# Layer 1 of a four-layer transformer stack: keys' feature map in one VectorE operation, and tiles 8 to 15 turned by crossbar DMAs

## The chip, the core and the metric

The kernel runs on one core of a Trainium2 chip. A core has TensorE (PE, the matrix unit), VectorE (DVE), ScalarE (ACT), GpSimd (POOL), SyncE (SP, which here issues every DMA) and 16 DMA engines. The metric is the time of one execution on the device in microseconds (us), as the median of a few runs.

## The reference

Four layers follow each other: A, B, A, B, with the same weights for both A layers and for both B layers. S = 2048 tokens, D = 576, H = 32 heads of 18, F = 4608, bf16 inputs.

```python
def _A_ref(x, wqkv, wo):                       # linear attention
    q, k, v = split_heads(x @ wqkv)
    phi = lambda t: jnp.where(t > 0, t + 1, jnp.exp(t)) + 1e-6
    pq, pk = phi(q), phi(k)
    kv = jnp.einsum("bhsd,bhse->bhde", pk, v)
    z = jnp.einsum("bhsd->bhd", pk)
    num = jnp.einsum("bhqd,bhde->bhqe", pq, kv)
    den = jnp.einsum("bhqd,bhd->bhq", pq, z)[..., None] + 1e-6
    return merge_heads(num / den) @ wo

def _B_ref(x, w1, b1, w2, b2):                 # MLP with its own layernorm
    h = _gelu(jnp.einsum("bsd,df->bsf", _layernorm(x), w1) + b1)
    return jnp.einsum("bsf,fd->bsd", h, w2) + b2

x = x + _A_ref(_layernorm(x), A_wqkv, A_wo)
x = x + _B_ref(_layernorm(x), B_w1, B_b1, B_w2, B_b2)
x = x + _A_ref(_layernorm(x), A_wqkv, A_wo)
x = x + _B_ref(_layernorm(x), B_w1, B_b1, B_w2, B_b2)
```

## The kernel before

The tokens are cut into 16 tiles of 128 (NT = 16). A tile of normalized rows is needed twice in an A layer. Turned (features on the partitions), it lies in `yT`, 5 chunks of 128 features by 2048 tokens, and feeds the projections to queries and keys. Unturned it is the stationary operand of the sums over tokens: instead of forming the values, the kernel sums rows times keys (`k2`, and a row of ones gives z) and multiplies by the value weights afterwards.

Layer 1 (li = 0) goes over the tiles in a loop written out by hand. `keys(t)` is two `k_half` calls, each 5 matmuls of 288 columns into PSUM. `pre_a1(t)` feeds a later tile to the layernorm pipe and ticks it. Then come one `q_proj` (5 matmuls of 512 columns) and `rows_by_keys(t, 0)` (5 matmuls: 4 chunks of rows into the accumulators accA and accB, and the tail of 64 features with the ones). TensorE's order is the order of the program, fixed by a chain of dependencies (`pe`). The order on DVE and ACT for the first tiles is written out (`in_order`, with names such as n0, ma00, e00, ca0).

The layernorm pipe (`LNPipe.tick`) takes each fed tile one stage further per tick: statistics (L397, L398 and L404 on DVE), variance plus epsilon (L415), the reciprocal root by a power on POOL (L433), minus mean times that (L436), the normalization (L444 on POOL from tile 4 on, L449 on DVE before), and stage 4, the turning. In layer 1 stage 4 is 5 TensorE transposes into PSUM (L500) and a copy to `yT` by ACT (L505). The last 64 features of a normalized tile are written to a ring of their own, `v_ring`, that has the ones beside them (`first_tail`), so a tile takes two normalizing operations. Tile t is fed in iteration t - 3 and turned in iteration t - 1.

The keys' feature map exists in two forms. `phi_from_psum` has two ACT passes (Exp at L554, Identity with a bias of 1 + 1e-6 at L555) and two DVE operations (L560, L562). `phi_by_dve` has one ACT pass (L537) and two DVE operations (L539, L541). The first half of the keys takes the first form, the second half the other.

All DMAs are issued by SP. In the beginning `chained` fixes their order: rows of x, the weights of layer 1, then `late_pieces` (w1 in 9 pieces with two tails each, wo, w2 in 6 pieces, b1), one piece per iteration in program order. A DMA waits on SP until the DMA eight before it has landed, and for the producer of its data.

In layers 2 and 4 (class `LayerB`) and in layer 3 nothing of this loop is used: rows are turned there by DVE in blocks of 32 and by DMAs through DRAM (`turn_rows`, `land`, L310, L325), and the unturned rows of layer 3 are loaded from DRAM (`load_row`, with the tails apart at L333). The loop of layer 3 has the same matmuls per tile (two `k_half`, one `q_proj`, one `rows_by_keys`) and no transposes.

Of the kernel before, what the change touches and what calls it, by code (L numbers as in the profile page):

```python
# [8 lines left out]
ALU = mybir.AluOpType  # L9
# [11 lines left out]
G = 5  # L21
# [9 lines left out]
HALF = D // 2  # L31
LAST_PARTS = (slice(0, 3 * P), slice(3 * P, D))
# [3 lines left out]
def build(tc, A_x, A_wqkv, A_wo, B_w1, B_b1, B_w2, B_b2, out, dbg=None, n_layers=4):  # L36
    nc = tc.nc
    dbg = dbg or {}
    with ExitStack() as ctx:
# [95 lines left out]
        NV = 2  # L135
        v_ring = [const.tile([P, G, P], BF16, name=f"v_ring{i}") for i in range(NV)]
        AHEAD = 4
        turned = const.tile([P, D // 32, TPC, 32], BF16, name="turned")
# [8 lines left out]
        def row_tile(name):  # L147
            return rows.tile([P, D], F32, name=name, tag="row")

        x0_tiles = {}  # L150

# [32 lines left out]
        def load_x0(t):  # L184
            if t % 2 == 0:
                x0_tiles["pair"] = rows.tile([P, 2, D], BF16, name="x0", tag="row")
            x0 = x0_tiles["pair"][:, t % 2, :]
            chained(nc.sync.dma_start(out=x0, in_=x_in[t * P:(t + 1) * P, :]))
            x0_tiles[t] = x0
# [31 lines left out]
        for vr in v_ring:  # L221
            nc.gpsimd.memset(vr[:], 0.0)
            nc.gpsimd.memset(vr[:].rearrange("p g c -> p (g c)")[:, 0:520].rearrange("p (t e) -> p t e", e=65)[:, :, 64:65], 1.0)
# [5 lines left out]
        def piece_w1(i):  # L229
            cs = slice(i * 512, (i + 1) * 512)  # L230
            chained(nc.sync.dma_start(out=w1_sb[:, 0:4, cs], in_=B_w1[0:4 * P, cs].rearrange("(k p) n -> p k n", p=P)))
            ts = slice(i * 256, (i + 1) * 256)
            for par in range(2):
                chained(nc.sync.dma_start(
                    out=w1_tail[64 * par:64 * (par + 1), ts].rearrange("k (f p) -> k f p", p=P),
                    in_=B_w1[4 * P:D, cs].rearrange("k (f two p) -> k f two p", two=2, p=P)[:, :, par, :]))
# [16 lines left out]
        def bias_casts():  # L253
# [4 lines left out]
                      [(lambda i=i: piece_w1(i)) for i in range(4, 9)] + [(lambda i=i: piece_w2(i)) for i in range(6)] + [piece_b1_dma]  # L258
# [6 lines left out]

        def tail_of(t):

            flat = v_ring[t // 8][:].rearrange("p g c -> p (g c)")
            return flat[:, (t % 8) * 65:(t % 8 + 1) * 65]

        def tails(c):
            flat = v_ring[c // 2][:].rearrange("p g c -> p (g c)")
            return flat[:, (c % 2) * 260:(c % 2 + 1) * 260].rearrange("p (t e) -> p t e", e=65)

        def first_tail(t, width=65):

            slot = 2 * (t % 8) + t // 8
            flat = v_ring[slot // 8][:].rearrange("p g c -> p (g c)")
            return flat[:, (slot % 8) * 65:(slot % 8) * 65 + width]
# [9 lines left out]
        def load_row(t):  # L289
            if t % 2 == 0:  # L290
                pair = rows.tile([P, 2, D], BF16, name="yrow_pair", tag="row")
                row_of[t], row_of[t + 1] = pair[:, 0, :], pair[:, 1, :]
            load = nc.sync.dma_start(out=row_of[t][:, 0:4 * P], in_=yrow_d[t // TPC, t % TPC].rearrange("j r d -> (j r) d")[:, 0:4 * P])
            if t >= 6:
                behind(load, "landed")
# [20 lines left out]
        def land(now=False):  # L316

            for it in list(landing):
# [11 lines left out]
                if kind == "A":  # L330
                    if c == NCB - 1:
                        sp_last["landed"] = landed.ins.name
                    tail = nc.sync.dma_start(out=tails(c)[:, :, 0:64],  # L333
                                             in_=yrow_d[c].rearrange("i j r d -> (j r) i d")[:, :, 4 * P:D])
                    behind(tail, "landed")
# [11 lines left out]
        class LNPipe:  # L347
# [11 lines left out]
            def tick(self, transposes=1):  # L359
                land()  # L360
                for it in list(self.items):
                    st = it["stage"]
                    if st == 4 and it["evac"] != "dma":
# [12 lines left out]
                    elif st == 0 and it["stats"] == "act":  # L376
# [7 lines left out]
                        continue  # L384
                    elif st == 0.5:
# [4 lines left out]
                        nc.gpsimd.tensor_scalar(out=u[:], in0=mv[:, 1:2], scalar1=(1.0 + EPS) / D, scalar2=EPS * EPS,  # L390
# [48 lines left out]
                    elif st in (2, 3) and it["kind"] == "A" and it["evac"] == "act":  # L439
                        xt, t = it["xt"], it["t"]  # L440
                        tail = first_tail(t)[:, 0:64]
                        if it["norm"] == "pool":
                            for out, cols in ((xt[:, 0:4 * P], slice(0, 4 * P)), (tail, slice(4 * P, D))):
                                norm = nc.gpsimd.tensor_scalar(out=out, in0=xt[:, cols], scalar1=it["rstd"][:, 0:1],  # L444
                                                               scalar2=it["nmr"][:, 0:1], op0=ALU.mult, op1=ALU.add)
                            pool_last["norm"] = norm.ins.name
                        else:
                            for name, out, cols in ((f"n{t}", xt[:, 0:4 * P], slice(0, 4 * P)), (f"nt{t}", tail, slice(4 * P, D))):
                                norm = named(name, nc.vector.tensor_scalar(  # L449
                                    out=out, in0=xt[:, cols], scalar1=it["mv"][:, 0:1], scalar2=it["rstd"][:, 0:1],  # L450
                                    op0=ALU.subtract, op1=ALU.mult))
# [31 lines left out]
                    elif st == 4:  # L483
                        t = it["t"]
                        first_layer = it["kind"] == "A" and it["evac"] == "act"
                        y = it["xt"] if first_layer else it["y"]
                        if it["evac"] == "dma":
                            turn_rows(y, t, it["kind"])
                            self.items.remove(it)
# [8 lines left out]
                        for k in range(KD):  # L498
                            block = first_tail(t, P) if first_layer and k == 4 else y[:, k * P:(k + 1) * P]
                            pe(nc.tensor.transpose(out=(tp if k < 3 else tp2)[:, k, :], in_=block, identity=ident[:]))  # L500
# [34 lines left out]
        def phi_by_dve(ps_ap, out_ap, rows, n, tag=None):  # L535
# [8 lines left out]
            if tag is not None:  # L544
                named("e" + tag, exp), named("mi" + tag, low), named("ma" + tag, top)

# [68 lines left out]
        def layer_A(li, next_kind, pre_a1=None):  # L615
# [34 lines left out]
            def k_half(t, half, defer=False):  # L650
# [5 lines left out]
                by_dve = half or li == 0 and t == 2  # L656

                def phi():
                    if (half, t // 2) not in self_k["pk"]:
                        self_k["pk"][(half, t // 2)] = blk.tile([P, D], BF16, name="pk", tag="blk")  # L660
                    pk = self_k["pk"][(half, t // 2)][:, (t % 2) * HALF:(t % 2 + 1) * HALF]
                    (phi_by_dve if by_dve else phi_from_psum)(kp[:, 0:HALF], pk, P, HALF,
                                                              tag=f"{t}{half}" if li == 0 and t < 4 else None)
                if defer:
                    return phi
                phi()

            def rows_by_keys(t, half, chunks=(4, 0, 1, 2, 3), done=True):
# [5 lines left out]
                pk = self_k["pk"][(half, t // 2)][:, (t % 2) * HALF:(t % 2 + 1) * HALF]  # L674
                for k in chunks:
                    dst = self_k["tail"][0:65, 0:HALF] if k == 4 else self_k["acc"][k // 2][:, k % 2, 0:HALF]
                    lhsT = (tail_of(t) if li > 0 else first_tail(t)) if k == 4 else row_of[t][:, k * P:(k + 1) * P]
                    pe(nc.tensor.matmul(dst, lhsT=lhsT, rhs=pk, start=(t == 0), stop=(t == NT - 1)))  # L678
                cols = slice(half * HALF, (half + 1) * HALF)
                if 4 in chunks and t == NT - 1:  # L680
                    nc.gpsimd.memset(zk[:, cols], 0.0)
                    nc.scalar.copy(out=k2[4][0:64, cols], in_=self_k["tail"][0:64, 0:HALF])
                    nc.scalar.copy(out=zk[64:65, cols], in_=self_k["tail"][64:65, 0:HALF])
                if not done:
                    return
                if t % 2:
# [7 lines left out]
                for i, copy in enumerate((nc.scalar.copy, nc.vector.tensor_copy)):  # L694
                    for j in range(2):
                        copy(out=k2[2 * i + j][:, cols], in_=self_k["acc"][i][:, j, 0:HALF])

            def last_rows_by_keys():

                parts = [ps_h.tile([P, 512], F32, name=name, tag="h") for name in ("z_rows", "k2_tail")]  # L700
                for size, part in zip((32, 64), parts):
                    n = P // size
                    for t in range(NT):
                        tail = tail_of(t) if li > 0 else first_tail(t)
                        lhsT = tail[:, 64:65].to_broadcast([P, 32]) if size == 32 else tail[:, 0:64]
# [3 lines left out]
                nc.scalar.activation(out=zk[:, HALF:D], in_=parts[0][:, 0:HALF], func=ACT.Identity, scale=1.0 / 32)  # L709
                nc.scalar.copy(out=k2[4][:, HALF:D], in_=parts[1][:, 0:HALF])  # L710
# [36 lines left out]
            def z_stage():  # L747
                zp = ps_h.tile([P, 512], F32, name="z_ps", tag="h")
                for g in range(G):
                    pe(nc.tensor.matmul(zp[0:GR[g], g:g + 1], lhsT=zk[:, GO[g]:GO[g] + GR[g]],  # L750
                                        rhs=(tail_of(0) if li > 0 else first_tail(0))[:, 64:65],
# [73 lines left out]
            if li == 0:  # L825
# [28 lines left out]
                in_order("s0a s0b g0 s1a s1b n0 nt0 g1 cd0 n1 nt1 s2a s2b g2 cd1 mi00 s3a n2 nt2 s3b ma00 g3 u3 mi10 s4a "  # L854
                         "mi11 n3 ma10 nt3 ma11 mi20 ma20 mi21 s4b ma21 g4 u4 mi01 ma01 s5a s5b mi30 g5 mi31 u5 ma30 ma31")
                in_order("ln0 re0 ln1 re1 ca0 e00 ca1 ln2 re2 id00 e01 e10 ca2 e11 id10 e20 e21 ca3 e31 e30 id30 ca4")
# [103 lines left out]
            for t in range(NT):  # L960
# [18 lines left out]
                if t == NT - 3:  # L979
                    warm_table(ACT.Gelu_apprx_tanh, act_last["copy"])  # L980
                state["wo"] = t
# [140 lines left out]
        def feed0(t, after=None):  # L1122
            lnp.feed(x0_tiles.pop(t), t, "A", l0_norm_eng(t), "act", after=after)
# [12 lines left out]
        def pre_a1_layer0(t):  # L1136
            if t + 3 < NT:
                feed0(t + 3, after=dve_last["phi"])
# [10 lines left out]
        for li, kind in enumerate(kinds):  # L1149
# [11 lines left out]
            else:  # L1161
                pe_chain.update(on=True)
# [50 lines left out]
```

## Time and profile before

| what | value |
|---|---|
| runs (us) | 760.68, 760.40, 760.71; median 760.68 |
| profiled execution: span | 758.4 us |
| PE busy | 753.2 us (99%) |
| PEld, DVE, ACT, POOL busy | 64%, 36%, 43%, 15% of the span |
| stretch 17.91 to 55.11 us (layer 1's loop, tiles 4 to 14): PE, DVE, ACT, POOL busy | 37.20, 31.41, 30.81, 25.59 of 37.20 us |
| DMA in that stretch | 0.99 of the 16 engines' time, 284 GB/s |
| granted TensorE clock | 1.00 in every stretch |

The page gives no time of the profiled execution but its span, from the first to the last recorded instruction; the median of the runs lies 2.3 us above it. Times of single instructions overlap: a matmul of 288 columns is recorded with 286 ns, but ten of them in a row start within 1.23 us. So rates are read from one group's start to the next group's start.

### The profile page before, as it was taken

How to read it: one execution, taken by the hardware profiler on the slowest of the kernel's cores; microseconds unless marked ns; L12 is line 12 of the kernel's file. 1: busy time of each engine (PE TensorE's matmuls, PEld its weight loads, DVE VectorE, ACT ScalarE, POOL GpSimd, SP SyncE). 2: the span in 40 equal slices, each digit the busy share in tenths (PEclk: the TensorE clock that was granted, in tenths of full speed). 3: DMA queues.
4: the chain of work that ended last, by engine and by line, in shares of the span. 5: the costliest groups of instructions: out<-in, count | busy, mean ns of one | idle time of the engine just before them, and what ended most of it. 6: DMA issues, size and time to landing. Idle time of an engine off the chain costs nothing.

```text
span 758.4 us, 15817 instructions
## 1 busy us (share of the span) xinstructions
PE 753.2 (99%) x6595; PEld 487.4 (64%) x6595; DVE 272.0 (36%) x685; ACT 328.7 (43%) x733; POOL 116.6 (15%) x196
## 2 busy tenths in 40 slices
PE   9999999999999999999999999999999999999998
PEld 5776754774477457646777777457646754774476
DVE  8876862136033503401367577600230131000000
ACT  6887656205600650263057666660174036205600
POOL 4840231002000301200100005300020020001000
PEclk9999999999999999999999999999999999999999
DMA  8994573026312711320404047530240033011000
GB/s 236 267 313 74 178 262 82 17 64 189 83 39 83 181 51 48 109 69 17 131 24 116 24 136 255 185 82 16 88 115 7 16 127 82 9 33 55 1 9 24
DMA packets 80977, 73.90 MB, mean 97 GB/s; under 512 B 36874, under 2 KB 65546, under 8 KB 80906
## 3 DMA queue, kind: packets, MB, share of 16 engines
q1 hardware_dynamic: 80906, 72.90, 33.0%
q8 instruction: 51, 0.84, 0.5%
q14 instruction: 20, 0.16, 0.1%
HBM read 48.10 MB, written 24.77 MB: 96 GB/s over the span
## 4 chain that ended last, share of the span: by engine, by line
PE 97%; DVE 1%; ACT 0%; issue 0%; DVEq 0%
PE m_ps L1104 36%; PE h_ps L1045 21%; PE hp_ps L1045 16%; PE q_ps L621 6%; PE k_ps L653 5%; PE wo_ps L933 5%; PE k_ps L678 4%; PE m_half L1104 1%; PE tp L500 1%; PE warm_ps L217 1%; PE k_tail L678 1%; PE kv_ps L719 0%; PE den_ps L769 0%; PE rden_ps L810 0%; PE kvwo_half L737 0%
## 5 line engine op out<-in xcount | busy, mean ns | idle before, releaser
L1104 PE MATMUL m_ps<-w_sb,hT 128*128 128x288 bf16 x2232 | 274.8, 286 | 0.0
L1104 PEld LDWEIGHTS <-hT 128*128 128x128 bf16 x2304 | 224.3, 98 | 60.4 <-issue 3.4
L1045 PEld LDWEIGHTS <-w_sb 64*128 64x128 bf16 x2304 | 124.5, 94 | 136.4 <-issue 1.9
L1045 PE MATMUL hp_ps<-yT,w_sb 64*128 64x512 bf16 x1152 | 178.0, 376 | 0.0
L1045 PE MATMUL h_ps<-yT,w_sb 64*128 64x512 bf16 x1152 | 148.0, 376 | 0.0
L1050 ACT COPY relay_sb<-relay_sb 128x1 f32<-128x1 f32 x144 | 28.5, 198 | 260.4 <-PE h_ps L1045 217.6
L1041 ACT ACTIVATE hT<-h_ps,b1T 128x512 bf16<-128x512 f32 x144 | 91.0, 683 | 44.1 <-PE h_ps L1045 44.1
L433 POOL TENSOR_TENSOR ln_rstd<-ln_u,neg_half 128x1 f32<-128x1 f32 x61 | 35.2, 577 | 439.9 <-DVE ln_u L415 218.0
L1041 ACT ACTIVATE hT<-hp_ps,b1T 128x512 bf16<-128x512 f32 x144 | 91.1, 692 | 0.0
L605 DVE TENSOR_TENSOR xbf<-m_ps,xo 128x576 bf16<-128x576 f32 x15 | 11.4, 757 | 213.5 <-PE m_ps L1104 213.5
L605 DVE TENSOR_TENSOR xo<-m_ps,xo 128x576 f32<-128x576 f32 x16 | 12.1, 757 | 172.6 <-PE m_ps L1104 172.6
L588 POOL TENSOR_TENSOR xo<-xo,b_bc 128x576 f32<-128x576 f32 x32 | 40.9, 1283 | 97.3 <-DMA xo<-x_d 58.4
L1045 PE MATMUL h_ps<-yT,w_tail 64*128 64x512 bf16 x144 | 54.1, 376 | 0.0
L1045 PE MATMUL hp_ps<-yT,w_tail 64*128 64x512 bf16 x144 | 54.1, 376 | 0.0
L621 PE MATMUL q_ps<-yT,wqkv_sb 128*126 128x512 bf16 (+1 forms) x200 | 49.3, 379 | 0.1
L653 PE MATMUL k_ps<-wqkv_sb,yT 128*128 128x288 bf16 x320 | 44.6, 286 | 0.2
L933 PE MATMUL wo_ps<-kvwo,pq 126*128 126x288 bf16 (+1 forms) x320 | 43.4, 286 | 0.3
L1045 PEld LDWEIGHTS <-w_tail 64*128 64x128 bf16 x288 | 27.1, 94 | 17.1
L653 PEld LDWEIGHTS <-yT 128*128 128x128 bf16 x320 | 31.0, 98 | 8.9 <-ACT yT L502 0.6
L933 PEld LDWEIGHTS <-pq 126*128 126x128 bf16 (+1 forms) x320 | 30.3, 97 | 9.1 <-issue 0.8
L621 PEld LDWEIGHTS <-wqkv_sb 128*126 128x126 bf16 (+1 forms) x200 | 25.7, 131 | 11.7 <-issue 0.5
L554 ACT ACTIVATE phi_e<-q_ps 126x512 bf16<-126x512 f32 (+1 forms) x40 | 23.9, 597 | 18.4 <-PE q_ps L621 16.8
(138 smaller groups left out, 591.6 us busy)
## 6 DMA issues: line engine op xcount, KB each, us to landing
xo<-x_d SPq DMA_DIRECT2D x48, 288.0 KB, 3.5
x_d<-xo SPq DMA_DIRECT2D x32, 288.0 KB, 2.6
xl<-x_d SPq DMA_DIRECT2D x24, 288.0 KB, 4.2
y_d<-turned SPq DMA_DIRECT2D x40, 144.0 KB, 3.1
w_sb<-in_B_w_dram SPq DMA_DIRECT2D x6, 864.0 KB, 10.4
yT<-y_d SPq DMA_DIRECT2D x10, 512.0 KB, 4.2
w_sb<-in_B_w_dram SPq DMA_DIRECT2D x9, 512.0 KB, 5.9
x_d<-xn SPq DMA_DIRECT2D x16, 288.0 KB, 3.3
```

Source lines behind the costliest of these rows:

```text
L433: nc.gpsimd.tensor_tensor(out=rstd[:], in0=it["u"][:], in1=neg_half[:], op=ALU.pow)
L554: exp = nc.scalar.activation(out=e_out, in_=ps_ap, func=ACT.Exp)
L588: nc.gpsimd.tensor_tensor(out=xo[:], in0=xo[:], in1=b2_bc[:], op=ALU.add)
L605: total = nc.vector.tensor_tensor(out=xn[:, cols].rearrange("p (h n) -> p h n", h=2), in0=halves, in1=xo[:, cols].rearrange("p (h n) -> p ...
L621: pe(nc.tensor.matmul(qp[0:GR[g], :], lhsT=wqkv_sb[:, k, GO[g]:GO[g] + GR[g]], rhs=yT[:, k, c * CA:(c + 1) * CA], start=(k == 0), stop=(k ...
L653: pe(nc.tensor.matmul(kp[:, 0:HALF], lhsT=yT[:, k, t * P:(t + 1) * P], rhs=wqkv_sb[:, k, D + half * HALF: D + (half + 1) * HALF], start=(k ...
L678: pe(nc.tensor.matmul(dst, lhsT=lhsT, rhs=pk, start=(t == 0), stop=(t == NT - 1)))
L933: pe(nc.tensor.matmul(wp[:, half, 0:HALF], lhsT=pq[(g, c)][0:GR[g], j * P:(j + 1) * P], rhs=kvwo[g][0:GR[g], half * HALF:(half + 1) * HALF ...
L1041: act_last["gelu"] = nc.scalar.activation(out=to, in_=ps, func=ACT.Gelu_apprx_tanh, bias=b1T[:, f:f + 1], scale=1.0).ins.name
L1045: mm = pe(nc.tensor.matmul(dst[n], lhsT=wt, rhs=mv, start=(seen[n] == 0), stop=(seen[n] == 8)))
L1050: relay = nc.scalar.copy(out=relay_sb[:, 1:2], in_=relay_sb[:, 0:1])
L1104: pe(nc.tensor.matmul(acc[half][:, 0:cols.stop - cols.start], lhsT=hT[f][:, j * P:(j + 1) * P], rhs=w2_sb[:, f, cols], start=(f == 0), sto ...
```

## The change

Three things change in layer 1, and some weights' loads with them.

The keys' feature map (`phi_of_first`): a row of ones in the weights (row 64 of chunk 4, key columns) meets a column of ones beside the rows, so the matmul gives k + 1. ACT takes exp(k + 1 - 1) with a bias of -1, and one DVE operation takes min(max(k + 1, 1), exp(k)). The 1e-6 is added to the sums over the tokens instead: a 289th column of ones beside the first half of the keys gives the sums of the rows, DVE makes `key_eps` of it (4 small operations), and the copies of the accumulators add it (`plus_eps`).

The rows: tiles are 640 wide with ones in the last 64 columns (`RW`), `v_ring` is gone, and a tile takes one normalizing operation. In layer 3 `load_row` loads all 576 columns and POOL sets the ones; the four loads of tails are gone. POOL sets the ones row of the weights back to zero after layer 1.

The turning: tiles 8 to 15 (`XB = 8`) take one crossbar transpose DMA each (`dma_start_transpose`, SBUF to SBUF, 128 x 640 bf16) in the place of 5 TensorE transposes and an ACT copy. Tiles from 8 on are fed one iteration earlier (iteration t - 4), and tiles 9, 12 and 15 have their statistics on ACT. On SP each transpose stands in the chain between two pieces of w1, and waits there for its tile's normalization.

The w1 tails are two loads instead of 18, and the last three pieces of w2 are issued in the last four tiles of the output projection of layer 1.

```diff
         def load_row(t):
             if t % 2 == 0:
-                pair = rows.tile([P, 2, D], BF16, name="yrow_pair", tag="row")
+                pair = rows.tile([P, 2, RW], BF16, name="yrow_pair", tag="row")
+                nc.gpsimd.memset(pair[:, :, D:RW], 1.0)
...
-                    tail = nc.sync.dma_start(out=tails(c)[:, :, 0:64],
-                                             in_=yrow_d[c].rearrange("i j r d -> (j r) i d")[:, :, 4 * P:D])
...
                         if it["norm"] == "pool":
-                            for out, cols in ((xt[:, 0:4 * P], slice(0, 4 * P)), (tail, slice(4 * P, D))):
-                                norm = nc.gpsimd.tensor_scalar(out=out, in0=xt[:, cols], scalar1=it["rstd"][:, 0:1],
-                                                               scalar2=it["nmr"][:, 0:1], op0=ALU.mult, op1=ALU.add)
+                            norm = nc.gpsimd.tensor_scalar(out=xt[:, 0:D], in0=xt[:, 0:D], scalar1=it["rstd"][:, 0:1],
+                                                           scalar2=it["nmr"][:, 0:1], op0=ALU.mult, op1=ALU.add)
...
+                        if it["evac"] == "xbar":
+                            chained(nc.sync.dma_start_transpose(out=yT[:, :, t * P:(t + 1) * P], in_=y[:, 0:DPAD]))
+                            self.items.remove(it)
+                            continue
...
+        def phi_of_first(ps_ap, out_ap, n, tag=None):
+            e = exp_tile(tag)[:, 0:n]
+            exp = nc.scalar.activation(out=e, in_=ps_ap, func=ACT.Exp, bias=neg_one[:, 0:1])
+            act_last["exp"] = exp.ins.name
+            top = nc.vector.scalar_tensor_tensor(out=out_ap, in0=ps_ap, scalar=1.0, in1=e, op0=ALU.max, op1=ALU.min)
...
+                if summed and t == NT - 1:
+                    for i in range(2):
+                        nc.vector.tensor_scalar(out=key_eps[:, 2 * i:2 * i + 2].unsqueeze(2),
+                                                in0=self_k["acc"][i][:, :, HALF:HALF + 1], scalar1=1e-6, scalar2=None,
+                                                op0=ALU.mult)
...
         def feed0(t, after=None):
-            lnp.feed(x0_tiles.pop(t), t, "A", l0_norm_eng(t), "act", after=after)
+            lnp.feed(x0_tiles.pop(t), t, "A", l0_norm_eng(t), "act" if t < XB else "xbar", after=after,
+                     stats="act" if t >= XB and t % 3 == 0 else "dve")
...
         def pre_a1_layer0(t):
-            if t + 3 < NT:
-                feed0(t + 3, after=dve_last["phi"])
+            for ahead in (3, 4) if t == 4 else (4,):
+                if t + ahead < NT:
+                    feed0(t + ahead, after=dve_last["phi"])
...
+                if li == 1:
+                    nc.gpsimd.memset(wqkv_sb[64:P, 4, D:2 * D], 0.0)
```

More of the change, by code (lines that the diff above doesn't have):

```diff
@@ L134, in build @@
         y_ring = [const.tile([P, DPAD], BF16, name=f"y_ring{i}") for i in range(NY)]
-        NV = 2
-        v_ring = [const.tile([P, G, P], BF16, name=f"v_ring{i}") for i in range(NV)]
+        neg_one = const.tile([P, 1], F32, name="neg_one")
+        key_eps = const.tile([P, 8], F32, name="key_eps")
         AHEAD = 4
+        XB = 8
         turned = const.tile([P, D // 32, TPC, 32], BF16, name="turned")
@@ L147, in row_tile @@
         def row_tile(name):
-            return rows.tile([P, D], F32, name=name, tag="row")
+            return rows.tile([P, RW], F32, name=name, tag="row")[:, 0:D]
         x0_tiles = {}
+        x0_pairs = []
         NOSYNC = mybir.DependencyInfo(mybir.DependencyClass.NoSync, mybir.DependencyReason.SCHED_ONLY)
@@ L185, in load_x0 @@
             if t % 2 == 0:
-                x0_tiles["pair"] = rows.tile([P, 2, D], BF16, name="x0", tag="row")
+                x0_tiles["pair"] = rows.tile([P, 2, RW], BF16, name="x0", tag="row")
             x0 = x0_tiles["pair"][:, t % 2, :]
-            chained(nc.sync.dma_start(out=x0, in_=x_in[t * P:(t + 1) * P, :]))
+            chained(nc.sync.dma_start(out=x0[:, 0:D], in_=x_in[t * P:(t + 1) * P, :]))
+            if t % 2 == 0:
+                x0_pairs.append(x0_tiles["pair"])
             x0_tiles[t] = x0
@@ L231, in piece_w1, with piece_w1_tail @@
             chained(nc.sync.dma_start(out=w1_sb[:, 0:4, cs], in_=B_w1[0:4 * P, cs].rearrange("(k p) n -> p k n", p=P)))
[L232 to L236, printed above, removed]
+        def piece_w1_tail(par):
+            chained(nc.sync.dma_start(
+                out=w1_tail[64 * par:64 * (par + 1), :].rearrange("k (f p) -> k f p", p=P),
+                in_=B_w1[4 * P:D, :].rearrange("k (f two p) -> k f two p", two=2, p=P)[:, :, par, :]))
         def piece_w2(i):
@@ L264, in build @@
         landing = []
[L266 to L279, printed above, removed]
         row_of = {}
@@ L362, in tick @@
                     st = it["stage"]
-                    if st == 4 and it["evac"] != "dma":
+                    if st == 4 and it["evac"] not in ("dma", "xbar"):
                         if transposes == 0 or state["wo"] < it["tp_at"]:
@@ L498, in tick @@
                         for k in range(KD):
-                            block = first_tail(t, P) if first_layer and k == 4 else y[:, k * P:(k + 1) * P]
-                            pe(nc.tensor.transpose(out=(tp if k < 3 else tp2)[:, k, :], in_=block, identity=ident[:]))
+                            pe(nc.tensor.transpose(out=(tp if k < 3 else tp2)[:, k, :], in_=y[:, k * P:(k + 1) * P],
+                                                   identity=ident[:]))
                         if first:
```

102 lines of the change are left out of this document (67 added, 35 removed).

## The prediction

> **What bounds the kernel now.** I read the page first: the engines' shares and the chain that ended last.
>
> ```profile
> span 758.4 us, 15817 instructions
> PE 753.2 (99%) x6595; PEld 487.4 (64%) x6595; DVE 272.0 (36%) x685; ACT 328.7 (43%) x733; POOL 116.6 (15%) x196
> ...
> PE 97%; DVE 1%; ACT 0%; issue 0%; DVEq 0%
> ```
>
> TensorE is busy 99% of the span, and 97% of the chain that ended last is TensorE. So work that leaves DVE or ACT brings nothing unless TensorE waits for it; work that leaves TensorE counts in full. The second view is TensorE's timeline in layer 1's loop, here tile 5:
>
> ```profile
> 21.18 1.39 PE L653 MATMUL k_ps<-wqkv_sb,yT 128*128 128x288 bf16 x10
> 22.40 0.39 PE L500 MATMUL tp<-ident,x 128*128 128x128 bf16 x4
> 22.62 0.22 PE L500 MATMUL tp<-ident,v_ring 128*128 128x128 bf16 x1
> 22.75 1.24 PE L621 MATMUL q_ps<-yT,wqkv_sb 128*126 128x512 bf16 x5
> 23.83 0.29 PE L678 MATMUL k_tail<-pk,v_ring 128*65 128x288 bf16 x1
> 23.95 0.65 PE L678 MATMUL k_ps<-pk,x 128*128 128x288 bf16 x4
> 24.44 1.39 PE L653 MATMUL k_ps<-wqkv_sb,yT 128*128 128x288 bf16 x10
> ```
>
> One tile takes 24.44 - 21.18 = 3.26 us: keys 1.22, transposes 0.35 (22.40 to 22.75), queries 1.08, sums 0.61. The chain in order of time shows the same loop in layer 3, where nothing is turned on TensorE:
>
> ```profile
> 388.86 1.23 PE k_ps L653 x10
> 390.09 1.08 PE q_ps L621 x5
> 391.78 1.23 PE k_ps L653 x10
> ```
>
> There a tile takes 391.78 - 388.86 = 2.92 us: exactly 0.34 us less, the transposes' stretch. Third, TensorE's start-up. Between the first keys (6.51) and tile 4's (17.91) it loses a little:
>
> ```profile
> 12.01 0.38 PE L500 MATMUL tp<-ident,x 128*128 128x128 bf16 x4 [0.18 <-DVE pk L541]
> ...
> 11.51 0.45 DVE L541 SCALAR_TENSOR_TENSOR pk<-k_ps,y_ring 128x288 bf16<-128x288 f32 x1
> ```
>
> The keys before it started at 10.44 and take 1.23, so TensorE was free at 11.67 and stood 0.34 us (recorded as 0.18, since ends are modelled) until DVE's feature map gave back a PSUM buffer. The median of the runs (760.68) lies 2.28 us above the span; I leave that part alone.
>
> **The change, part by part.** *Forty transposes leave TensorE.* Tiles 8 to 15 were turned in iterations 7 to 14, so eight iterations fall from 3.264 to 2.92 us: 8 x 0.345 = 2.76 us gained, if each turned tile is in `yT` when its keys start. The 16 sums with a 289th column (80 matmuls, 1/288 of 0.123 us each) cost 0.03.
>
> *The new period must be met by the others.* DVE per tile is now about 2.3 us (statistics 1.1, queries 0.7, two feature maps of 0.45 back to back 0.37), ACT 1.6, and 2.8 with two passes over a row for tiles 9, 12 and 15; both are under 2.92 (in the stretch before they were busy 31.4 and 30.8 of 37.2). POOL has 0.55 + 0.26 + 0.86 for a tile, some 0.6 of masks and 0.1 for a ones column: 2.4.
>
> *Start-up.* DVE loses the four tails' normalizations (0.2 each net) and the separate minimum of each feature map (0.2). The feature map that held the transposes at 12.01 comes about 0.5 us earlier by that count, behind which 0.34 us of standing goes; what is late next is TensorE itself. Against it stands a new set of ones in the weights (1 x 576, near the 0.48 of L647, plus its gap of 0.15) ahead of the first statistics. DVE had 0.46 free there, so about 0.2 is late; but the first copy to `yT` waits for tile 1's root behind tile 0's normalization, which lost its 0.2 us tail, and 0.08 is left. The 0.07 by which iteration 7 is longer than the others (a 0.48 us set of ones on DVE ahead of the keys' map) goes too. Sum: 0.34 + 0.07 - 0.08 = 0.33 gained; bounds 0 and 0.7 (all 0.73 of standing before tile 4).
>
> *Eight crossbar DMAs.* The trace has none, so latency and pace are bounded by the nearest rows. When is a tile's normalization done? Before, POOL's rows for tiles 7 and 8 are these:
>
> ```profile
> 23.31 0.77 POOL L444 TENSOR_SCALAR x<-x,ln_rstd,ln_nmr 128x512 bf16<-128x512 bf16 x1
> ...
> 26.57 0.77 POOL L444 TENSOR_SCALAR x<-x,ln_rstd,ln_nmr 128x512 bf16<-128x512 bf16 x1
> ```
>
> Tile 8 is now fed with tile 7, and POOL does it right behind: 24.2 less 0.33, then 0.55 to 0.8 + 0.35 + 0.86 gives 25.9. Its keys start at 31.04 - 0.33 - 0.345 = 30.4 (iteration 8 started at 31.04). So a turned tile may take about 4.5 us; the later ones have that or more, since POOL's 2.4 us is below 2.92. The nearest durations, from the page and the DMA view:
>
> ```profile
> y_d<-turned SPq DMA_DIRECT2D x40, 144.0 KB, 3.1
> ...
> w_sb<-in_B_w_dram SPq DMA_DIRECT2D x9, 512.0 KB, 5.9
> ...
> out_dram<-xbf SPq DMA_DIRECT2D x15, 144.0 KB, 1.8
> yrow_pair<-yrow_d SPq DMA_DIRECT2D x16, 128.0 KB, 3.1
> yT<-y_d SPq DMA_DIRECT2D x16, 64.0 KB, 5.4
> ```
>
> They reach from 1.8 us (a plain store, idle queue) to 5.9 (512 KB, full queue). I take 3.1, the row nearest in kind: 144 KB read from SBUF in pieces of 128 elements. It is under 4.5, so the cost is nothing; what hides it is two iterations of TensorE. At 5.9 the first tile would be 1.4 us late, once. SP's issue of such a DMA took about 0.6 (four in 2.46), and with one w1 piece (0.4 to 0.6) SP needs some 1.2 of 2.92 us per tile. A gain from the transfers themselves is excluded: they can only be in time.
>
> The Trainium skill ("Advanced Engine Details and Errata", X-Bar Transpose) says that transposing DMAs are as fast as regular ones; by it the cost is nothing too. Its page "VectorE: DVE Perf Modes", in The three transpose paths, gives 1309 ns for one 128 x 128 block by crossbar; five of them one after the other would be an estimated 6.5 us per tile, and that is weighed under the rivals.
>
> *What is queued behind the transposes.* SP now waits for POOL at each, and the w1 pieces behind wait with it. After the last (some 46 us) there are still one w1 piece, the tails, b2, three w2 pieces, b1 and the first residual rows, 4.7 MB; at the 284 GB/s of the stretch before that is 16.5 us, so 62.5, about where b1 landed before (63.8). The residual rows are used at 80, b1 at 102, w2's last pieces (issued from about 93 on, 10.4 us each) at 141. All covered by tens of us.
>
> *After the loop and layer 3.* Four small DVE operations (0.2 each) stand before the accumulators' copies, which ended at 58.9; TensorE needs the banks at 60.76. Hidden; without that 1.8 us of cover it would be 0.8. In layer 3 POOL's eight sets of ones (0.2 each) stand among the roots; tile 15's root (397.15) had 11 us of idle time before it. Nothing.
>
> **Sum.** 2.76 + 0.33 - 0.03 = 3.06. The span goes from 758.4 to 755.3, the median from 760.68 to 757.6.
>
> **The rivals.** *The transposes go one after the other, slowly (slower).* If a tile occupies the crossbar path for s us and the tiles do not overlap, tile 15 lands at 25.9 + 8s, and its keys want it at 30.4 + 7 x 2.92 = 50.8. From s = (50.8 + 3.06 - 25.9) / 8 = 3.5 us on, the change loses. At the 5.4 us of the slowest small row above, tile 15 lands at 69.1: 18.3 late, 757.6 + 18.3 = 775.9. For it: the trace has no such DMA, and these 640 pieces per tile are small. Against: four stores of 576 such pieces are issued within 2.46 us and land 3.1 us after their issue, so plain ones do overlap. By the skill's 1309 ns per block, s would be 6.5 and the estimate 784.7; no row here bears that out. Chance 0.20.
>
> *Late, but overlapping.* Latency between 4.5 and 6.5 us: the first tile stalls TensorE by up to 2 us and the rest follow in step: 758.6 to 759.6, typically 759.0. The rows with 5.4 and 5.9 speak for it; these are loads from DRAM in a full queue, while SP's waits for POOL keep this queue short. Chance 0.12.
>
> *The transposes were not what the loop waits for.* POOL or ACT, which had 0.3 to 0.8 us spare per tile, becomes the bound at about 3.2 us, and only the start-up gain stays: 760.3. Against it is layer 3's loop, whose DVE and ACT are as busy (33.9 and 34.3 of 47.3) at 2.92; but POOL is nearly idle there. Chance 0.08.
>
> **How the numbers follow.** Measurement of this kernel tells about 0.2% from no change, which is 1.5 us: faster is below 759.2, slower above 762.2. The forecast (757.6; its own range 756.9 to 758.6: below by the start-up's other 0.37, 0.2 of TensorE's idle time from 60 to 100 us and half the spread of the runs, 0.15; above by the start-up's 0.33 and small stalls) gets 0.60. Faster: 0.60 and two thirds of the late case, 0.68. Same: the rest of it and the third rival, 0.12. Slower: 0.20. The range runs from 756.9 over both middle cases to 761.5 and leaves the slow case out.
>
> **What would show it.** Right: keys starting every 2.92 us from iteration 7 on, crossbar DMAs landing within 4.5 us of their issue, no idle TensorE before L653, the gap at 12.01 gone. Wrong: TensorE idle before the keys of tiles 8 to 15, released by a DMA into `yT`, or SP's issues of the transposes lasting 2 us and more, or POOL's rows for a tile ending in the iteration of its keys.

## The result, and the profile after

| what | before | after |
|---|---|---|
| runs | 760.5 us (760.35 to 760.82, 20 runs) | 761.55 us (761.24 to 762.27, 20 runs) |
| ratio, 95% interval | | 1.0014 [1.0007, 1.002] |
| span of the profiled execution | 758.4 us | 759.6 us |
| tile 4's keys start | 17.91 | 17.92 |
| tile 15's keys start | 53.89 | 54.52 |

The change makes the kernel 1.05 us slower; I had forecast 3.06 us faster. The page of the changed kernel:

```profile
span 759.6 us, 15684 instructions
PE 750.6 (99%) x6555; PEld 484.3 (64%) x6555; DVE 262.7 (35%) x642; ACT 328.1 (43%) x722; POOL 115.3 (15%) x219
...
PE 94%; POOL 2%; ACT 2%; DVE 2%; issue 1%; POOLq 0%; DVEq 0%; ACTq 0%
```

TensorE has 40 instructions and 2.6 us of work less, as it should, and the span is 1.2 us longer. The chain says where to look: TensorE's share fell from 97% to 94%, and POOL, ACT and DVE, which had 1% together, now have 6%. In the loop TensorE waits, where before it did not.

These are rows of TensorE's timeline after (start, duration, idle time and what ended it):

```profile
23.93 1.24 PE L626 MATMUL q_ps<-yT,wqkv_sb 128*126 128x512 bf16 x5 [0.60 <-DVE pk L547]
...
29.39 0.28 PE L700 MATMUL k_tail<-pk,x 128*65 128x289 bf16 x1 [0.68 <-POOL pk L664]
...
39.10 0.28 PE L700 MATMUL k_tail<-pk,x 128*65 128x289 bf16 x1 [0.53 <-POOL pk L664]
...
39.71 1.39 PE L658 MATMUL k_ps<-wqkv_sb,yT 128*128 128x288 bf16 x10
...
42.63 1.39 PE L658 MATMUL k_ps<-wqkv_sb,yT 128*128 128x288 bf16 x10
```

The last two rows are the forecast come true: 42.63 - 39.71 = 2.92 us for a tile, and nowhere in this trace does TensorE wait for a crossbar DMA. The first three are what I did not see: the queries wait for DVE's feature map, the sums for a 0.1 us set of ones on POOL. From one keys' start to the next, by iteration:

| iteration | 4 | 5 | 6 | 7 | 8 | 9 | 10 | 11 | 12 | 13 | 14 | sum |
|---|---|---|---|---|---|---|---|---|---|---|---|---|
| before | 3.27 | 3.26 | 3.26 | 3.34 | 3.26 | 3.26 | 3.27 | 3.26 | 3.27 | 3.26 | 3.27 | 35.98 |
| after | 3.74 | 3.96 | 4.39 | 2.92 | 2.92 | 3.86 | 2.92 | 2.92 | 3.12 | 2.93 | 2.92 | 36.60 |

Iterations 4 to 6, in which TensorE still transposes, lose 2.30 us; iterations 7 to 14 gain 1.68 of the forecast 2.83 (0.07 of it iteration 7's), since 9 and 12 are long. The loop loses 0.62 of the span's 1.2 us. Another 0.25 us is lost between the first `m_ps` of layer 2 and that of layer 4, where layer 3 lies: the changed kernel took 372.07 us there and the kernel before 371.82; after the change TensorE waits 0.41 us for POOL there, at 467.86. Of the variants below, all with the same layer 3, five took 371.80 to 371.95 (e1 to e4, e7) and the nine others 372.06 to 372.24. So this part comes and goes with something that no run here isolates. The last 0.3 lies behind the last DVE operation, where only the last store is left, and stays unexplained.

### The profile page after: what moved, and what is told of

The parts are those of the page before. It is cut to its first block, busy times and chain, and to the rows that moved or that the text cites. A ratio compares the mean times of both kernels' runs of the same rounds, so it can differ in the third digit from the quotient of the medians.

```text
span 759.6 us, 15684 instructions
## 1 busy us (share of the span) xinstructions
PE 750.6 (99%) x6555; PEld 484.3 (64%) x6555; DVE 262.7 (35%) x642; ACT 328.1 (43%) x722; POOL 115.3 (15%) x219
## 4 chain that ended last, share of the span: by engine, by line
PE 94%; POOL 2%; ACT 2%; DVE 2%; issue 1%; POOLq 0%; DVEq 0%; ACTq 0%
PE m_ps L1140 36%; PE h_ps L1081 21%; PE hp_ps L1081 16%; PE q_ps L626 5%; PE k_ps L658 4%; PE wo_ps L967 4%; PE k_ps L700 4%; PE m_half L1140 1%; POOL ln_rstd L428 0%; PE k_tail L700 0%; PE kv_ps L752 0%; ACT turned L847 0%; PE rden_ps L843 0%; PE den_ps L802 0%; POOL x L437 0%
```

## The experiments

Theory 1: POOL works in order, and each keys' column of ones stands in its queue behind the normalization of later tiles, which waits for ACT where ACT does the statistics. Theory 2: ACT's two passes over a row (tiles 9, 12, 15) stand ahead of the keys' exponentials. Theory 3: the new map gives a PSUM buffer back only when DVE has read it; before, ACT did so for the first half of the keys. Times are compared with those of the kernel before on the same chip.

### What the changed kernel loses: the ones on POOL, the statistics on ACT

e1: the ones are set once, in seven fixed tiles.

```diff
+ pk_ring = [turned_flat[:, 320 * i:320 * i + HALF + 1] for i in range(7)]   # ones set once, at the start
...
- pk = self_k["pk"][(0, t)] = blk.tile([P, D], BF16, name="pk", tag="blk")
- nc.gpsimd.memset(pk[:, HALF:HALF + 1], 1.0)
+ pk = self_k["pk"][(0, t)] = pk_ring[t % 7]
```

> The changed kernel, but the ones beside the first half of the keys are set once, in seven places that the keys' tiles use in turn; POOL's 16 one-column sets in the loop are gone. Theory 1 (POOL's queue): TensorE's waits before the sums of tiles 6, 9 and 12 (0.83, 0.70 and 0.20 us in the changed kernel's trace) go, about 1.7 us: 0.7 us faster than the kernel before, 1.7 faster than the changed one. Theory 2 (PSUM buffers and the ACT queue hold everything anyway): the wait only moves to DVE's feature map, at most 0.4 us comes back.

e2: all statistics on DVE.

```diff
- stats="act" if t >= XB and t % 3 == 0 else "dve")
+ stats="dve")
```

> The changed kernel, but the statistics of tiles 9, 12 and 15 stay on DVE. Theory 2 (ACT's passes over a row delay the keys' exp): the wait of the queries of tile 5 shrinks from 0.7 to about 0.3 us and that of tile 9 (0.25) goes; POOL's root of tiles 9 and 12 no longer waits for ACT, so part of the 1.5 us before the sums goes too: 0.7 to 1.5 us faster than the changed kernel. Rival (the passes are covered): within 0.2 us of the changed kernel, or slower because DVE has two more tiles' statistics.

e5: both edits.

> Edits one and two together: the columns of ones are set once at the start in seven fixed places (no set of ones in POOL's queue during the loop), and the statistics of tiles 9, 12 and 15 are VectorE's. Theory 1 (POOL's queue and ScalarE's passes are one loss counted twice: once the statistics are VectorE's, the sums wait for POOL no more): iterations 4 and 5 stay at 3.75 and 3.55 us, iteration 6 falls from 3.71 to 3.55, all later ones at 2.92; the sums end 0.2 us earlier than with the statistics moved alone, and the time is within 0.3 us of that kernel's 759.15. Theory 2 (two separate losses): the two gains add up, 0.6 + 1.0, to about 758.5, and then an iteration with a transpose has to come below 3.55.

| kernel | time (us) | before | ratio | iterations 4, 5, 6 | 9 | 12 |
|---|---|---|---|---|---|---|
| e1 | 759.61 | 760.19 | 0.9992 [0.9984, 1.0001] | 3.74, 3.96, 3.55 | 3.17 | 2.92 |
| e2 | 759.15 | 760.19 | 0.9988 [0.998, 0.9997] | 3.75, 3.55, 3.71 | 2.92 | 2.92 |
| e5 | 759.01 | 760.2 | 0.999 [0.9982, 0.9999] | 3.75, 3.55, 3.55 | 4.27 | 2.92 |

Each edit alone brings back more than the whole loss of 1.05 us (e1's interval just reaches no change). e2 brings back 2.1, more than the 0.7 to 1.5 expected. The ones cost 0.84 us in iteration 6, 0.69 in 9 and 0.20 in 12; the statistics on ACT 0.41 in iteration 5, 0.68 in 6, 0.94 in 9 and 0.20 in 12. The two sums are not to be added: for the most part it is one chain. The changed kernel's chain in order of time, into the sums at 39.10, shows it:

```profile
34.76 0.77 ACT ln_dump L372 x2
35.58 0.35 issue
35.93 0.87 ACT ln_dump L382 x2
36.80 0.08 issue
36.88 0.20 POOL ln_u L385
37.08 0.07 issue
37.15 0.55 POOL ln_rstd L428
37.81 0.28 POOL ln_nmr L431
38.09 0.09 issue
38.18 0.82 POOL x L437
39.10 0.28 PE k_tail L700
```

ACT's two passes over tile 12's row end at 36.80, POOL makes root, shift and normalization of it until 39.00, and only then sets the column of ones, for keys whose map needs nothing of all that. Take away the ones (e1) or what POOL waits for (e2), and it is gone; so Theory 1 holds, and Theory 2 in that ACT's passes feed it and cost iteration 5 directly. Together (e5) the gains do not add up to 758.5; iterations 4 to 6 stop at 3.55 and above. The 4.27 of iteration 9 has another cause (below).

### Why 3.55: the feature map holds a PSUM buffer

e3 is the new map without the turning, all 16 tiles by TensorE.

```diff
- XB = 8
+ XB = 16
...
- for ahead in (3, 4) if t == 4 else (4,):
+ for ahead in (3,):
```

> The changed kernel with all 16 tiles turned by TensorE, fed as in the kernel before: the new feature map, rows and weights' loads without the crossbar. Theory 3 (with the transposes in the loop the four small PSUM buffers are short, and the new map holds the keys' buffers until DVE comes, where ACT let go of them before): queries wait 0.4 to 0.8 us in each of the iterations 4 to 14, 3 to 6 us slower than the kernel before. Rival (only POOL's queue and the ACT passes of the changed kernel matter): within 0.5 us of the kernel before.

It takes 764.15 us against 760.19, ratio 1.0053 [1.004, 1.0065], and nearly every iteration 3.55 us (iteration 4 3.74, 7 4.00): 0.29 more than before. Its waits (engine, line, waited for: us in total, times, longest):

```profile
PE q_ps L626 <- DVE pk L547: 2.7, 11, 0.6
```

Eleven times the queries wait for DVE's map. If a held buffer is the cause, ACT's release of before must bring it back. e7 does that in e3 from tile 4 on, e11 adds the preset ones of e1, and e6 does it in e5 in iterations 4 to 6 alone.

```diff
+ if 4 <= t < 7:                      # e7, e11: t >= 4
+     exp = nc.scalar.activation(out=e, in_=kp[:, 0:HALF], func=ACT.Exp, bias=neg_one[:, 0:1])
+     kept = nc.scalar.copy(out=a, in_=kp[:, 0:HALF])
+     top = nc.vector.scalar_tensor_tensor(out=pk[:, 0:HALF], in0=a, scalar=1.0, in1=e, op0=ALU.max, op1=ALU.min)
```

> The new feature map alone (all 16 tiles turned by TensorE), with ScalarE's copy of the first half from tile 4 on, as in the kernel before it. Theory 3 (buffers held until VectorE comes): the period falls from 3.55 to 3.26 us in all iterations and the time to that of the kernel before, 760.2 plus or minus 0.4. Rival (ScalarE's longer exponential, or VectorE's order): the period stays at 3.55 or above, 764.1 or more.

> The new feature map alone with ScalarE's copy from tile 4 on (763.55; iterations at 3.34 and four at 3.9 to 4.6 in which POOL's set of ones was late), and the ones set once at the start. Theory 1 and 3 together (POOL's queue and held buffers are all that the map costs): all iterations at 3.26 to 3.35, the row of sums at 59.3 to 60.0, the time 760.5 to 761.2. Rival (the map has a third cost): 762 or more.

> As the kernel with both edits, and in iterations 4 to 6 (those in which TensorE still transposes a tile) ScalarE makes the exponential and a bf16 copy of the first half's keys, as it did before, so that their PSUM buffer comes free when ScalarE is through; VectorE's one operation then reads the copy in SBUF. Theory 3 (the transposes and queries wait for one of the small PSUM buffers, which the new map holds until VectorE's operation has read it): iterations 4 to 6 go back to 3.26 us each, the row of sums is reached at about 56.4 instead of 57.6 us, and the time is 1.1 us below the kernel with both edits, about 757.9 where the kernel before is at 760.2. Rival (the loss comes from ScalarE, whose exponential with a bias tensor is recorded 0.5 instead of 0.41 us): a further pass on ScalarE makes it no better, iterations 4 to 6 stay at 3.55 or rise by up to 0.4 each, 759.0 to 760.2.

e7: 763.55 us, ratio 1.0035 [1.0023, 1.0048]; eight iterations at 3.34 or 3.35, but two at 3.86 and the last at 4.63, where the sums wait 1.1 us for POOL's ones once more (POOL itself waits 3.3 us for the load of b1). e11: 761.76 us against 760.38, 1.0018 [1.0009, 1.0027], and all eleven iterations at 3.34 or 3.35; it is 0.6 above the 761.2 expected at most, 0.3 of it outside the span (see e14). e6: iterations 4 to 6 at 3.35, 3.35, 3.34 where e5 had 3.75, 3.55, 3.55. So Theory 3 holds: a further pass on ACT made the loop 0.2 us per tile faster. DVE's own operation is no shorter with the copy (0.46 us in e3 and in e11 where it does not wait), so what the pass changed is when the buffer comes free. The expected 3.26 was not reached. The remaining 0.08 fits one row that was never on my list: the exponential of half a tile's keys before, then after:

```profile
L537 ACT ACTIVATE phi_e<-k_ps 128x288 bf16<-128x288 f32 x8 | 3.3, 410 | 0.0
```

```profile
L545 ACT ACTIVATE phi_e<-k_ps,neg_one 128x288 bf16<-128x288 f32 x18 | 8.8, 503 | 3.4 <-PE k_ps L658 2.2
```

With the bias tensor it takes 0.503 instead of 0.410 us, and the buffer comes free 0.09 later. No kernel varied that by itself.

### The turning alone, and a transpose that lands late

e4 has the transposes with the feature map of before, e8 in addition the statistics on DVE.

```diff
- phi_of_first(kp[:, 0:HALF], pk[:, 0:HALF], HALF, ...)
+ (phi_by_dve if half or t == 2 else phi_from_psum)(kp[:, 0:HALF], pk, P, HALF, ...)   # no ones row, no key_eps
```

> The changed kernel with the old feature map of the keys (no ones row, no 289th column, no small term on the sums): crossbar transposes, rows and loads alone. Theory 3: the whole 2.76 us of the transposes come, less what the ACT passes and the doubled statistics of iteration 4 cost: 2 to 3 us faster than the kernel before. Rival (the crossbar DMAs or the earlier feeding cost something that hides in the changed kernel): less than 1 us faster, with TensorE waiting before the keys of tiles 8 to 15.

> The crossbar transposes alone with the feature map of before, and the statistics of tiles 9, 12 and 15 on VectorE. In the kernel with the transposes alone, iterations 6 and 7 took 3.88 and 3.32 us behind ScalarE's passes for tile 9, iteration 8 was on time, and in the profiled execution one of the sixteen landings of tile 10's transpose came 2.1 us after the others (1.0 us of waiting). Theory (ScalarE's passes cost the turning its gain; the late landing is chance): iterations 4 to 6 at 3.26 to 3.3, all later ones at 2.92, the row of sums at 56.4 us, the time 2.4 to 2.8 us below the kernel before, 757.4 to 757.8. Rival 1 (POOL's normalizations, two tiles fed in iteration 4, are the late ones): iteration 6 stays near 3.9, 758.3 to 758.9. Rival 2 (the transposes land late in general): waits for a transpose in more than one iteration, no better than 758.9.

e4: 758.85 us against 760.19, 0.9987 [0.9978, 0.9996], 1.3 us faster where 2 to 3 were expected. e8: 758.22 against 760.2, 0.9977 [0.9968, 0.9985], 2.0 faster where 2.4 to 2.8 were expected, iterations 4 to 6 at 3.26 or 3.27, all later ones at 2.92 but iteration 7 (3.74). So the turning does what was forecast of it once ACT's passes are gone. e4's profiled execution has a wait that no other kernel so far had shown:

```profile
38.85 1.40 PE L657 MATMUL k_ps<-wqkv_sb,yT 128*128 128x288 bf16 x10 [1.04 <-DMA yT<-x]
```

Tile 10's transpose was issued at 31.68. The trace records sixteen landings for each transpose. Fifteen of this one's are recorded at 36.58 to 36.73, the last at 38.81, with most of those of the `wo` load that SP issues right behind it (38.47 to 38.82). e5 and e6 show the same tile with two landings of the sixteen at 39.15 and at 39.21; it made e5's iteration 9 4.27 us long and e6's 5.28. In e6's profiled execution a second loss followed the wait of 2.20 us: iteration 10 (39.26 to 43.87) has no wait in it and yet took 4.61 us instead of 2.92, with a granted clock of 0.63; behind the shorter waits of e4 (1.04 us) and e5 (1.2) the clock was 1.00. The late landing is not in every execution: e6's runs reach from 758.06 to 762.58, median 760.14, 0.9998 [0.9988, 1.0009], so that the gain of its loop is lost again. Two suspects came at that time, the load of `wo` (648 KB) and a 16 KB fetch of instructions at 33 to 35 us. e9 moves `wo` ahead of all transposes in e8, e12 behind tile 14's, and e10 is e6 with `wo` ahead.

```diff
- late_pieces = [piece_w1(0..3)] + [piece_wo] + [piece_w1(4..8)] + ...
+ late_pieces = [piece_wo] + [piece_w1(0..8)] + ...                      # e9, e10
+ late_pieces = [piece_w1(0..7)] + [piece_wo] + [piece_w1(8)] + ...     # e12
```

> As the kernel with the transposes alone and the statistics on VectorE, and the two loads of wo (567 and 81 KB), which SP issues right behind the transpose of tile 10, go ahead of all pieces of w1 and so ahead of all transposes. In three profiled executions one or two of the sixteen landings of tile 10's transpose came 2.1 us after the others, together with the landings of wo, and keys of tile 10 waited 1.0 to 2.2 us. Theory 4 (the load of wo behind it makes the transpose land late): no execution has the late landing, all runs lie within 0.7 us, median 757.9 (757.6 to 758.3), and no wait for a transpose in the profile. Rival (the 16 KB fetch of instructions, which came at 33.5 to 35.3 us in those executions, holds up one of the sixteen engines): the times stay in two groups 1.4 us apart, median 758.2, some at 759.5.

> The kernel with preset ones, statistics on VectorE and ScalarE's copy in iterations 4 to 6 (760.14, its runs from 758.06 to 762.58, its profiled execution with 2.2 us of waiting for the transpose of tile 10), with wo's loads ahead of the transposes. Theory 4: the scatter goes, all runs at 757.9 to 758.5, the change as a whole then 2 us below the kernel before. Rival (instruction fetch): scatter as before, median 759 to 760.

> As the transposes alone with the statistics on VectorE, wo's loads moved the other way: behind the transpose of tile 14, with pieces of w1 behind tile 10's. Theory 4: tile 10's transpose is on time in all executions and tile 14's (or 15's) is the one that may land late, so that times still fall in two groups. Rival (instruction fetch at 33 to 35 us): the late landing stays with tile 10 or 11.

e9: 758.31 us (758.06 to 758.56), 0.9971 [0.996, 0.9983]. e10: 758.41 (758.28 to 758.9), 0.9973 [0.9963, 0.9983]. e12: 758.28 (757.89 to 759.09), 0.9972 [0.9961, 0.9982]: tile 10 is on time there too, but no second group behind tile 14 showed (one of its seven runs lies 0.6 us above the next). Eight of e6's twelve runs lie above 759.9 us and none of e10's nine; three of e8's eleven lie 1.1 us above its others, and none of e9's six. So moving `wo` away from tile 10 removes the scatter.

It does not remove the late landing. In e10's trace, with `wo` far ahead, one landing of tile 10 is recorded at 36.81, 1.57 us after the other fifteen; tile 10's keys start at 37.04, so it costs nothing. And the other suspect fits all traces. A landing of tile 10 came more than 1.5 us behind the others in e1, e4, e5, e6 and e10, where the 16 KB fetch of instructions began at 34.05 to 34.66 us. In the seven other kernels with transposes it came with the others, and there the fetch began at 33.45 to 33.60 (e8, e9, e12, e13, e14), at 35.29 (e2) or at 37.13 (the changed kernel). With `wo` directly behind, the landing was 2.1 us late in e4, e5 and e6 and 1.64 in e1; in e2, e8 and the changed kernel it was not late at all. So the rival stands: when the fetch comes may decide whether a landing is late, and `wo` may add to it. No run here moved the fetch, so the cause stays open.

### What is late next: DVE in the loop, ACT at the start

e9's iteration 7 still takes 3.78 us. Its waits name DVE:

```profile
PE k_tail L693 <- DVE pk L565: 0.7, 1, 0.7
```

e13 is e9 with the queries' ones (0.48 us on DVE, once in four iterations) on POOL; e14 is e10 with the ones row of the weights set by POOL, for the start-up.

```diff
- (nc.gpsimd if li > 0 else nc.vector).memset(pq[(g, c)][96:P, 0:CA], 1.0)
+ nc.gpsimd.memset(pq[(g, c)][96:P, 0:CA], 1.0)                 # e13
...
- nc.vector.memset(wqkv_sb[64:65, 4, D:2 * D], 1.0)
+ nc.gpsimd.memset(wqkv_sb[64:65, 4, D:2 * D], 1.0)             # e14
```

> The transposes alone, statistics on VectorE, wo's loads first (758.31), and the ones of the queries' tiles in the loop (32 x 512, 0.48 us and a gap of 0.16 on VectorE, once in four iterations) set by POOL. In that kernel iteration 7 took 3.78 us, its sums waiting 0.70 us for VectorE's last keys, behind that set of ones and the statistics of a tile. Theory (VectorE is short in an iteration of 2.92 us by what stands in it besides its own tile): iteration 7 falls to 2.92 to 3.1, the time by 0.6 to 0.8, to 757.5 to 757.7. Rival (POOL, now with 0.5 us more, normalizes a tile late): iteration 8 or 9 loses as much, 758.2 or more.

> The kernel with preset ones, statistics on VectorE, ScalarE's copy in iterations 4 to 6 and wo first (758.41), and the row of ones in the weights set by POOL, out of VectorE's way at the start. The first transpose started at 5.55 us in all kernels with the row on VectorE, at 5.24 to 5.32 in those without it, and tile 4's keys at 17.92 to 18.26 against 17.60 to 17.86. Theory 5 (the row's 0.54 us on VectorE is what the start-up loses): the first transpose at 5.26, tile 4's keys at 17.6 to 17.8, the time 0.3 us lower, about 758.1. Rival (ScalarE's exponential with a bias tensor, 0.50 instead of 0.41 us for each half, in the start-up's chain): the first transpose at 5.26, but tile 4's keys still at 17.9 or later, 758.4.

e13: 757.93 us against 760.43, 0.9966 [0.9953, 0.9978]. Iteration 7 falls to 3.01, but 8 and 9 rise to 3.18 and 3.22: DVE is short there, as the theory says, and POOL right behind it, as the rival says; 0.2 us of iteration 7's 0.86 is won in these three iterations. e14: 757.94 us against 760.43, 0.9964 [0.995, 0.9978]. The first transpose starts at 5.21 instead of 5.55, and tile 4's keys still at 18.07, as the rival says. Its chain in order of time at the start shows what comes next:

```profile
6.78 0.83 PE k_ps L661 x5
7.61 0.02 issue
7.63 0.50 ACT y_ring L548
8.13 0.38 ACT yT L501
8.51 0.00 issue
8.51 0.44 DVE turned L550
8.95 0.01 issue
8.96 0.44 DVE x L444
9.40 0.05 issue
9.45 0.45 PE tp L498 x5
```

Here the exponential of 0.50 us stands in the chain from the first keys to tile 2's transposes. Before, the same stretch of the chain was DVE's from 6.02 to 11.97. So the start-up is not shorter; it changed the engine. That the longer exponential is what holds it up is not shown: e13 has the old map and no row of ones, its chain goes through ACT in the same place with an exponential of 0.41 us, and its tile 4's keys start at 18.04.

e14's time is nevertheless 0.47 lower than e10's. Only 0.2 of that is in the span (medians over the runs 756.2 and 756.4). The rest lies outside the span, 1.73 us in e14 and 2.04 in e10, which the profile does not show. This part is 1.93 to 2.04 us in all five other kernels with the preset ones (e1, e5, e6, e10, e11) and 1.69 to 1.80 in all the rest whose runs have a recorded span. So the preset ones go with 0.2 to 0.3 us more there, except in e14, and nothing here shows why.

e13 and e14 beat both kernels: 2.5 us faster than before, 3.5 faster than the change. e14 keeps all parts of the change, and only their places differ (statistics, ones and the row moved, ACT's release in three iterations, `wo` first).

## Why the prediction was wrong

**The step that failed is "The new period must be met by the others".** I summed each engine's work over a tile (DVE 2.3, ACT 2.8 at most, POOL 2.4 us, all under 2.92) and costed it at nothing. The sums were not far off: in iterations 7, 8, 10 and 11 of the changed kernel, which have no wait, DVE was busy 1.9 to 2.2 us, POOL 1.8, and ACT 1.4, or 2.7 to 2.9 with a row's passes, and the period is 2.92. (The terms given for DVE, 1.1 + 0.7 + 2 x 0.37, make 2.5 and not 2.3, also under 2.92.) What the sums leave out is order. POOL's 0.1 us of ones per tile was in my sum as 0.1; in the queue it stood behind a normalization that waited for ACT, and cost 0.84, 0.69 and 0.20 us of TensorE's time in iterations 6, 9 and 12 (1.73 in all, by e1). ACT's 2.8 us in an iteration was "under 2.92", and its passes still came ahead of the exponentials (0.41 in iteration 5 by e2, and POOL's lateness).

**A term was missing: the feature map in iterations 4 to 6.** I took DVE's fewer instructions as a gain or nothing. But the map of before let ACT give back the first half's buffer, and the new one leaves both to DVE: 0.29 us in each iteration that still has a transpose (e3). In e5, where the ones and the statistics are out of the way, iterations 4 to 6 are 0.48 + 0.29 + 0.29 = 1.06 us longer than before. My own reading of the start-up named just this wait, a transpose held until DVE's feature map gave back a PSUM buffer, and I did not ask where else it would occur.

**Start-up: 0.33 forecast, -0.01 measured** (17.92 against 17.91). The stall at 12.01 did go: the transposes there start at 11.92, without a wait. What comes earlier is late by as much: the first transposes start at 5.55 instead of 5.26, tile 2's at 9.30 instead of 9.05. "What is late next is TensorE itself" was wrong: between the first keys and tile 2's transposes the chain goes through ACT, its exponential and its copy to `yT` (e14, and e13 with the old map). The two maps do not separate clearly here: tile 4's keys start at 17.60 to 18.04 in the kernels with the old map (17.91 before the change and 18.04 in e13; the expectation of e14 names 17.60 to 17.86) and at 17.92 to 18.26 in those with the new one.

**The main term was right.** 8 x 0.345: where nothing waits, an iteration takes 2.92, and e10 and e14 have the eight at 23.5 us against 26.2 before. Of the forecast 3.06 for the whole, e14 has 2.5.

**The crossbar DMAs** were forecast at 3.1 us, with 4.5 us before the tile's keys. In the changed kernel the eight tiles landed 2.75 to 4.96 us after their issue: four near the forecast (2.75 to 3.15), three at 4.2, and tile 15 at 4.96, beyond the 4.5 named as the sign of being right, yet all in time; SP's issue took 1.21 to 1.33 us, not the 0.6 I took, and SP had room for it. The slow serial rival (0.20) is out: tile 8's packets went through in 0.94 us (27.02 to 27.96). By the figure of the Trainium skill's page "VectorE: DVE Perf Modes" (The three transpose paths) a tile would be an estimated 6.5 us; this trace does not agree. The Trainium skill's page "Advanced Engine Details and Errata" (X-Bar Transpose) calls these transfers as fast as regular ones, and for the landing on an idle queue this trace agrees: 2.75 us for tile 8, beside 1.8 to 3.1 for the 144 KB rows of before. "Late, but overlapping" (0.12) showed only in kernels that were otherwise faster (e4, e5, e6); in the changed kernel tile 10 landed at 35.61, 4.1 us before its keys.

**"POOL or ACT becomes the bound" (0.08)** named the right engines with the wrong mechanism and price: not a period of 3.2 everywhere, but three iterations that lose 2.30 us, one (9) that loses 0.60 and one (12) that keeps 0.15 of its 0.35. At 760.3 it was nearest to the 761.55.

## What to carry to other kernels

A sum of work per engine shows only that a period is possible; follow each small instruction in its queue, and ask what the one ahead of it waits for. When an edit lets a faster engine do in one pass what two did, ask who gives the buffer back afterwards, and when: here an extra ACT pass made the loop faster. When a gain leaves a DMA little time to spare, look at all of its landings and at everything that moves beside it, the next large load and the fetch of instructions too: one late landing of sixteen holds up the whole tile.

## What was not expected of the hardware

An exponential from PSUM (128 x 288) with a bias tensor took 0.503 us, without one 0.410. A crossbar transpose of 128 x 640 bf16 took SP 1.21 us to issue, twice a plain load's 0.57, and was recorded as 640 packets of 256 bytes. One or two of its sixteen landings could come 1.6 to 2.1 us after the others, in five of the twelve kernels' traces that have such DMAs. Behind a wait of TensorE of 2.20 us (e6) the next 4.61 us had a granted clock of 0.63.
